# Four parts of w_in decoded ahead of the attention loop, and alpha and the gate's columns in one transfer

## The chip, the cores and the metric

One core of a Trainium2 chip runs the whole program. The metric is the device time of one execution in microseconds (us). The engines are TensorE (PE in the rows; PEld is its weight load), VectorE (DVE), ScalarE (ACT), GpSimd (POOL) and SyncE (SP), whose queue issues nearly all transfers.

## The reference

Attention with a window of 32 and 32 global rows for each of 4 x 8 heads, then a dense layer of two matrices with a leaky activation, then a layer of eight experts with a gate. w_in and w_out come as 64-bit floats, the rest as 32-bit.

```python
def _attn_ref(q_l, k_l, v_l, q_g, k_g, v_g):
    B, H, Sl, D = q_l.shape                      # 4, 8, 512, 64; q_g, k_g, v_g have 32 rows
    window = 32
    scale = 1.0 / np.sqrt(D)
    k_all = np.concatenate([k_g, k_l], axis=2)
    v_all = np.concatenate([v_g, v_l], axis=2)
    out_g = np.matmul(sm(scale * np.matmul(q_g, k_all.transpose(0, 1, 3, 2))), v_all)
    s_ll = scale * np.matmul(q_l, k_l.transpose(0, 1, 3, 2))
    mask = np.abs(pos[:, None] - pos[None, :]) <= window
    s_ll = np.where(mask, s_ll, -1000000000.0)
    s_lg = scale * np.matmul(q_l, k_g.transpose(0, 1, 3, 2))
    a_l = sm(np.concatenate([s_lg, s_ll], axis=-1))
    out_l = np.matmul(a_l, np.concatenate([v_g, v_l], axis=2))
    return np.concatenate([out_g, out_l], axis=2)

def _moe_ref(x, w_in, w_out, alpha):             # x 2176 x 512, w_in 512 x 2048, w_out 2048 x 512
    h = x @ w_in
    g = np.maximum(h, 0.0) + alpha * np.minimum(h, 0.0)
    return g @ w_out

def _moe2_ref(x, w_gate, w1, w2):                # w_gate 512 x 8; eight experts of 512 x 1024 x 512
    logits = x @ w_gate
    ...                                          # highest logits first, 272 tokens for each expert
    for e in range(E):
        mask = assigned == e
        out[mask] = np.maximum(x[mask] @ w1[e], 0.0) @ w2[e]
    return out
```

## The kernel before

The attention runs over 16 units (a batch and a pair of heads), two units at a time: a **pair** p of units is loaded by `load(p)` (queries and keys `qk`, values `vv`) and worked off in four **steps** of 128 query rows. Step n (four for each pair, counted through from 0) does: scores on PE (L366, tile `s`), mask and row minimum on DVE (L372, four instructions `sc`), exponentials on ACT (L374, four, tile `pr`), the division on DVE (L379, L380, L386), transposes on PE (L392) with a copy on ACT (L394), and the product with the values on PE (L403) with a copy on ACT (L405). The 32 global rows of a pair are done between the steps (L419 to L454). The output of a pair lies in `xb`.

The first matrix product (`gemm`, L172 for h and L203 for y) takes chunks of 272 tokens. It starts when two pairs are done (`done[0] < UPB - 1`), that is behind step 7 and the rest of its chain; then `xh` and `xl` (L73 on DVE, 128x1088) are split off `xb`, and from there PE alternates between attention and `gemm` until all eight pairs are done.

w_in and w_out must be **decoded** from 64-bit to 32-bit floats and split into a high and a low part. `win_part(pool, hf, i)` and `wout_part` do one **part** of 128 x 512: a transfer of 512 KB into `raw` (L79, three buffers), the absolute value on ACT (L82), four instructions on DVE (L83, L85, L86, L87), a cast on ACT (L72) and a subtraction on POOL (L73). The first half of the layer has 8 parts of w_in and 8 of w_out, 16 in all. Before the change four of w_in are written into the first attention loop, one behind every sixth piece of work; the other four and the eight of w_out follow in the loop with `gemm`. Alpha (2048 numbers, one for each column of w_in) and the gate's columns (512 x 8) are loaded behind the first loop, by a transfer each, from their own layout in memory.

The order of instructions on each engine isn't the order of the code: the tile framework reorders by a timeline of its own (`schedule_with_timeline_sim=True`) when the program is built. Each engine then runs its instructions strictly in that order, and a transfer in SP's queue waits for the ones ahead of it.

Of the kernel before, what the change touches and what calls it, by code (L numbers as in the profile page):

```python
# [9 lines left out]
F32 = mybir.dt.float32  # L10
# [15 lines left out]
def tile_attention_moe_moe(ctx: ExitStack, tc: tile.TileContext, qkw, vw,  # L26
                           w_in, w_out, alpha, w_gate, w1, w2, out):
    nc = tc.nc
    V, A, P, T = nc.vector, nc.scalar, nc.gpsimd, nc.tensor
# [33 lines left out]
    Lm = cp.tile([128, NT, E], F32, name="Lm")  # L63
    al = cp.tile([128, KF], F32, name="al")
    al1 = cp.tile([128, KF], F32, name="al1")
    wg = cp.tile([128, KD, 32], F32, name="wg")
    wop = cp.tile([128, KH, 32], F32, name="wop")
    P.memset(wg, 0.0)
    P.memset(wop, 0.0)
# [220 lines left out]
    with ExitStack() as at:  # L290
# [31 lines left out]

        def load(p):
            for cut in range(2 if p == 0 else 1):
                for u in (2 * p, 2 * p + 1):
# [5 lines left out]
                    part = slice(None) if p else (slice(0, QS + kpos(6)), slice(QS + kpos(6), None))[cut]  # L331
                    nc.sync.dma_start(out=d["qk"][:, part], in_=qkw[u, :, part])
            for u in (2 * p, 2 * p + 1):
                U[u]["v"] = ld.tile([128, NQ, 2 * D], F32, name="vv")
                nc.sync.dma_start(out=U[u]["v"].rearrange("p i d -> p (i d)"), in_=vw[u])
# [164 lines left out]

        load(0)
        mask = mk.tile([128, 3, KW], F32, name="mask")
# [15 lines left out]
        UPB = H // 2  # L518
        parts = [(win_part, i) for i in range(2 * KD)]
        att = attention()  # L520
        n = 0
        while done[0] < UPB - 1:
            next(att)
            n += 1
            if n >= 6 and n % 6 == 0 and len(parts) > KD:
                f, i = parts.pop(0)
                f(dc, 0, i)
        nc.sync.dma_start(out=al, in_=alpha.rearrange("(f p) -> p f", p=128))
        V.tensor_scalar(al1, al, -1.0, 1.0, op0=OP.mult, op1=OP.add)
        nc.sync.dma_start(out=wg[:, :, :E], in_=w_gate.rearrange("(k p) e -> p k e", p=128))  # L530
        parts += [(wout_part, i) for i in range(KH)]
# [686 lines left out]

_INS = ['qk', 'v', 'moe_w_in', 'moe_w_out', 'moe_alpha', 'moe2_w_gate', 'moe2_w1', 'moe2_w2']
_OUTS = [((2176, 512), 'float32')]  # L1220
# [39 lines left out]


# [24 lines left out]
```

## Time and profile before

| | us |
|---|---|
| median of 3 runs (869.75 to 871.96) | 869.96 |
| the profiled execution | 870.56 |
| its span | 868.8 |
| PE busy in the span | 820.1 (94%) |
| DVE busy | 466.8 (54%) |
| ACT busy | 389.6 (45%) |
| POOL busy | 348.5 (40%) |

The span is that of the trace; the execution lasts 1.8 us longer than it. A share of busy time is a mean over stages: in the first 40th of the page's slices PE is busy six tenths, later nine and more. The stages that the change touches lie in the first 110 us.

### The profile page before, as it was taken

To read this page: it belongs to the slowest core of one execution; us is meant where nothing else is said; L and a number is where in the kernel's file an instruction comes from. 1 tells how busy PE (TensorE), PEld (TensorE's weight loads), DVE (VectorE), ACT (ScalarE), POOL (GpSimd) and SP (SyncE) were. 2 spreads that over 40 slices of the span, in tenths; PEclk is the share of its full clock that TensorE was granted. 3 is DMA by queue.
4 is the path that set the end of the run, shared out by engine and by line. 5 is a ranking of instruction groups with operands and counts; after the bars stand their busy time and mean duration, and the time that the engine had idled before them with its cause. 6 is when DMAs were issued, how large, how long until landed. Compare 5 with 4: busy or idle time off the path is not lost. (4 is left out here: it accounts for less than half of the span.)

```text
span 868.8 us, 21017 instructions
## 1 busy us (share of the span) xinstructions
PE 820.1 (94%) x8380; PEld 746.0 (86%) x8380; DVE 466.8 (54%) x1654; ACT 389.6 (45%) x970; POOL 348.5 (40%) x300
## 2 busy tenths in 40 slices
PE   6699799999988999999999999999899999999995
PEld 4478688888988999988898899999699989999995
DVE  4789945463288734133333457666575776722120
ACT  5577646464454543232322434341254535444431
POOL 1214412020145534200000638470598868779601
PEclk9589999999999999999999999999999999999998
DMA  9777715631345302201311217242366655666300
GB/s 345 230 255 272 261 38 192 212 124 47 95 134 183 114 26 79 72 7 53 103 52 54 78 54 267 64 131 65 100 198 217 168 177 153 174 187 185 111 25 37
DMA packets 50441, 115.94 MB, mean 133 GB/s; under 512 B 6759, under 2 KB 23399, under 8 KB 48295
## 3 DMA queue, kind: packets, MB, share of 16 engines
q1 hardware_dynamic: 47447, 105.68, 37.8%
q0 software_dynamic: 2896, 8.92, 3.1%
q8 instruction: 66, 1.08, 0.5%
q14 instruction: 32, 0.26, 0.1%
HBM read 96.76 MB, written 17.83 MB: 132 GB/s over the span
## 5 line engine op out<-in xcount | busy, mean ns | idle before, releaser
L172 PE MATMUL h<-xh,win 128*128 128x272 f32 x768 | 162.3, 295 | 3.9 <-DVE g L178 2.5
L73 POOL TENSOR_TENSOR m<-raw,m 128x1024 fp32r<-128x1024 f32 x64 | 152.4, 2402 | 21.6 <-ACT m L72 21.3
L172 PEld LDWEIGHTS h<-xh,win 128*128 128x128 f32 x768 | 124.9, 188 | 12.0 <-issue 4.9
L73 POOL TENSOR_TENSOR glo<-g,ghi 128x272 fp32r<-128x272 f32 x64 | 55.4, 866 | 150.8 <-ACT ghi L72 150.7
L203 PE MATMUL y<-ghi,wout 128*128 128x272 f32 x512 | 112.5, 298 | 2.5 <-ACT wout L72 1.3
L172 PE MATMUL h<-xl,win 128*128 128x272 f32 x384 | 111.3, 290 | 1.4 <-DVE xl L73 1.4
L1104 PE MATMUL h<-gr,wout 128*128 128x272 f32 x768 | 110.7, 295 | 0.0
L73 POOL TENSOR_TENSOR gr<-gb,gr 128x272 fp32r<-128x272 f32 x64 | 48.0, 772 | 153.2 <-ACT gr L72 144.6
L977 PE MATMUL h<-xsh,m 128*128 128x272 f32 x512 | 107.4, 297 | 1.3 <-ACT xsh L72 1.3
L993 PE MATMUL h<-hh,m 128*128 128x272 f32 x512 | 103.2, 293 | 0.0
L1104 PEld LDWEIGHTS h<-gr,wout 128*128 128x128 f32 x768 | 99.2, 188 | 0.9 <-ACT gr L72 0.4
L203 PEld LDWEIGHTS y<-ghi,wout 128*128 128x128 f32 x512 | 84.3, 188 | 8.3 <-issue 4.0
L177 ACT ACTIVATE neg<-h 128x272 f32<-128x272 f32 x128 | 50.5, 395 | 90.1 <-PE h L172 89.7
L977 PEld LDWEIGHTS h<-xsh,m 128*128 128x128 f32 x512 | 83.1, 190 | 1.9 <-ACT xsh L72 1.4
L993 PEld LDWEIGHTS h<-hh,m 128*128 128x128 f32 x512 | 81.7, 188 | 0.7 <-issue 0.5
L72 ACT CAST m<-raw 128x1024 fp32r<-128x1024 f32 x64 | 65.4, 1049 | 29.1 <-DMA raw<-in_moe_w_dram 28.9
L993 PE MATMUL h<-hl,m 128*128 128x272 f32 x256 | 75.5, 295 | 0.0
L203 PE MATMUL y<-glo,wout 128*128 128x272 f32 x256 | 73.8, 293 | 1.8 <-POOL glo L73 1.5
L977 PE MATMUL h<-xsl,m 128*128 128x272 f32 x256 | 74.9, 292 | 0.5 <-DVE xsl L73 0.5
L172 PEld LDWEIGHTS h<-xl,win 128*128 128x128 f32 x384 | 72.3, 188 | 2.4 <-DVE xl L73 1.9
L178 DVE SCALAR_TENSOR_TENSOR gb<-neg,al,h 128x272 f32<-128x272 f32 x64 | 31.6, 496 | 76.5 <-ACT neg L177 66.0
L374 ACT ACTIVATE pr<-sc,mx 128x128 f32<-128x128 f32 x128 | 50.1, 393 | 30.6 <-DVE mx L372 30.4
(231 smaller groups left out, 1517.2 us busy)
## 6 DMA issues: line engine op xcount, KB each, us to landing
raw<-in_moe_w_dram SPq DMA_DIRECT2D x64, 512.0 KB, 3.8
vv<-in_v_dram SPq DMA_DIRECT2D x16, 1024.0 KB, 8.0
qk<-in_qk_dram SPq DMA_DIRECT2D x14, 720.0 KB, 8.5
raw<-in_moe_w_in_dram SPq DMA_DIRECT2D x16, 512.0 KB, 4.4
raw<-in_moe_w_out_dram SPq DMA_DIRECT2D x16, 512.0 KB, 4.2
xs<-xb SPq DMA_DIRECT2D x16, 272.0 KB, 8.8
xpart<-xd SPq DMA_DIRECT2D x32, 136.0 KB, 1.7
xb<-xs SPq DMA_DIRECT2D x8, 544.0 KB, 4.0
```

Source lines behind the costliest of these rows:

```text
L72: a = A.copy(hi, src)
L73: return a, (lo_eng or V).tensor_tensor(lo, src, hi.bitcast(F32), op=OP.subtract)
L172: T.matmul(ps, wi[:, w, k, fs], x[:, k], start=i == 0, stop=i == 3 * KD - 1)
L177: A.activation(out=neg, in_=ps, func=AF.Relu, scale=-1.0)
L178: epi[0] = V.scalar_tensor_tensor(g, neg, al1[:, hf * KH + f:hf * KH + f + 1], ps, op0=OP.mult, op1=OP.add)
L203: T.matmul(ps, wo[:, w, f, ds_], x[:, f], start=i == 0, stop=i == 3 * KH - 1)
L374: A.activation(out=d["pr", j][:, ii], in_=sc, func=AF.Exp, bias=d["mx", j][:, ii:ii + 1], scale=-1.0, accum_out=d["sm", j][:, ii:ii + 1])
L977: T.matmul(ps, d["w1"][:, w, kk, fs], x[:, kk], start=i == 0, stop=i == 3 * KD - 1)
L993: T.matmul(ps, d["w2"][:, w, f, ms], x[:, f], start=i == 0, stop=i == 3 * K3 - 1)
L1104: T.matmul(ps[j], wo[:, w, f, ds_], x, start=f == 0 and a == 0, stop=f == KH - 1 and a == 2)
```

## The change

The first four parts of w_in are issued inside `load(0)`: two behind the first cut of `qk` of pair 0, two behind its second cut, ahead of the values. They are no longer in the attention loop. Alpha and the gate's columns lie in one array `gate` of 128 x 144, which is laid out ahead of the launch, with zeros where the gate's columns are padded from 8 to 32; it takes one transfer, and the clearing of `wg` on POOL (L68) is gone. `al` and `wg` are views of the one tile. Line numbers behind L320 move by 2 to 5.

```diff
@@ -61,11 +61,11 @@
     Lm = cp.tile([128, NT, E], F32, name="Lm")
-    al = cp.tile([128, KF], F32, name="al")
+    ag = cp.tile([128, KF + KD * 32], F32, name="ag")
+    al = ag[:, :KF]
     al1 = cp.tile([128, KF], F32, name="al1")
-    wg = cp.tile([128, KD, 32], F32, name="wg")
+    wg = ag[:, KF:].rearrange("p (k e) -> p k e", e=32)
     wop = cp.tile([128, KH, 32], F32, name="wop")
-    P.memset(wg, 0.0)
     P.memset(wop, 0.0)
@@ -320,7 +320,7 @@
-        def load(p):
+        def load(p, between=()):
             for cut in range(2 if p == 0 else 1):
                 for u in (2 * p, 2 * p + 1):
...
                     nc.sync.dma_start(out=d["qk"][:, part], in_=qkw[u, :, part])
+                for f in between[2 * cut:2 * cut + 2]:
+                    f()
             for u in (2 * p, 2 * p + 1):
@@ -498,7 +500,9 @@
-        load(0)
+        parts = [(win_part, i) for i in range(2 * KD)]
+        load(0, [lambda i=i: win_part(dc, 0, i) for _, i in parts[:KD]])
+        del parts[:KD]
@@ -516,18 +520,11 @@
         UPB = H // 2
-        parts = [(win_part, i) for i in range(2 * KD)]
         att = attention()
-        n = 0
         while done[0] < UPB - 1:
             next(att)
-            n += 1
-            if n >= 6 and n % 6 == 0 and len(parts) > KD:
-                f, i = parts.pop(0)
-                f(dc, 0, i)
-        nc.sync.dma_start(out=al, in_=alpha.rearrange("(f p) -> p f", p=128))
+        nc.sync.dma_start(out=ag, in_=gate)
         V.tensor_scalar(al1, al, -1.0, 1.0, op0=OP.mult, op1=OP.add)
-        nc.sync.dma_start(out=wg[:, :, :E], in_=w_gate.rearrange("(k p) e -> p k e", p=128))
         parts += [(wout_part, i) for i in range(KH)]
@@ -1259,6 +1256,14 @@
+def lay_gate(alpha, w_gate):
+    import numpy as _np
+    E = w_gate.shape[1]
+    wg = _np.zeros((128, w_gate.shape[0] // 128, 32), w_gate.dtype)
+    wg[:, :, :E] = w_gate.reshape(-1, 128, E).transpose(1, 0, 2)
+    return _np.concatenate([alpha.reshape(-1, 128).T, wg.reshape(128, -1)], axis=1)
```

**SP's queue, from its start.** Each row is a transfer, with its tiles and its shape (L79 brings a part's `raw`). Before:

```order
L332 DMA qk<-in_qk_dram 128x416 x2
L332 DMA qk<-in_qk_dram 128x1024 x2
L335 DMA vv<-in_v_dram 128x2048 x2
L332 DMA qk<-in_qk_dram 128x1440 x2
L335 DMA vv<-in_v_dram 128x2048 x2
L79 DMA raw<-in_moe_w_in_dram 128x1024 x3
L528 DMA al<-in_moe_alpha_dram 128x16x1
L530 DMA wg<-in_moe_w_gate_dram 128x4x8
L332 DMA qk<-in_qk_dram 128x1440 x2
L79 DMA raw<-in_moe_w_in_dram 128x1024 x4
```

And with the change, from the same place:

```order
L332 DMA qk<-in_qk_dram 128x416 x2
L79 DMA raw<-in_moe_w_in_dram 128x1024 x2
L332 DMA qk<-in_qk_dram 128x1024 x2
L79 DMA raw<-in_moe_w_in_dram 128x1024
L337 DMA vv<-in_v_dram 128x2048 x2
L332 DMA qk<-in_qk_dram 128x1440 x2
L337 DMA vv<-in_v_dram 128x2048 x2
L526 DMA ag<-in_gate_dram 128x144
L79 DMA raw<-in_moe_w_in_dram 128x1024 x3
L332 DMA qk<-in_qk_dram 128x1440 x2
```

Three parts stand ahead of the values of pair 0, two of them ahead of the second cut of its queries and keys; the fourth part waits for a buffer and comes behind the loads of pair 1.

**ACT, from its start.** L82 is the absolute value of a part and L72 its cast; `pr` are the exponentials of a step (L374 before, L376 with the change). Before:

```order
L374 ACTIVATE pr,sm<-sc,mx 128x128 x8
L394 COPY pt<-t 128x512
L424 ACTIVATE gsc,gmx<-gsc,gmx 128x544
L374 ACTIVATE pr,sm<-sc,mx 128x128 x4
L394 COPY pt<-t 128x512
L374 ACTIVATE pr,sm<-sc,mx 128x128
```

With the change:

```order
L82 ACTIVATE mag<-raw 128x512
L376 ACTIVATE pr,sm<-sc,mx 128x128 x4
L82 ACTIVATE mag<-raw 128x512
L72 CAST win<-mag 128x512
L82 ACTIVATE mag<-raw 128x512
L72 CAST win<-mag 128x512
L376 ACTIVATE pr,sm<-sc,mx 128x128 x2
L396 COPY pt<-t 128x512
L72 CAST win<-mag 128x512
L376 ACTIVATE pr,sm<-sc,mx 128x128 x3
```

The first part's absolute value stands ahead of the exponentials of step 0, and the three first parts are done before step 2.

**DVE, between the exponentials' division of step 4 and the scores of step 5.** `mag` are the four instructions of a part, `sm` and `pr` the division, `xb<-go` the global rows of pair 0, `sc,mx` the scores. Before, behind the scores of step 4:

```order
L83 TENSOR_SCALAR mag<-mag 128x512
L85 TENSOR_SCALAR mag<-mag 128x512
L86 SCALAR_TENSOR_TENSOR mag<-raw,mag 128x512
L379 TENSOR_SCALAR sm<-sm 128x4
L83 TENSOR_SCALAR mag<-mag 128x512
L87 SCALAR_TENSOR_TENSOR mag<-raw,mag 128x512
L380 RECIPROCAL sm<-sm 128x4
L85 TENSOR_SCALAR mag<-mag 128x512
L529 TENSOR_SCALAR al_70<-al 128x16
L386 TENSOR_SCALAR pr<-pr,sm 128x128 x4
L86 SCALAR_TENSOR_TENSOR mag<-raw,mag 128x512
L87 SCALAR_TENSOR_TENSOR mag<-raw,mag 128x512
```

These are two of the four parts that stand there; the other two follow, around the copy of `xb<-go`, up to the scores of step 5.

With the change, at the same place:

```order
L527 TENSOR_SCALAR al_70<-ag 128x16
L381 TENSOR_SCALAR sm<-sm 128x4
L382 RECIPROCAL sm<-sm 128x4
L388 TENSOR_SCALAR pr<-pr,sm 128x128 x4
L83 TENSOR_SCALAR mag<-mag 128x512
L85 TENSOR_SCALAR mag<-mag 128x512
L86 SCALAR_TENSOR_TENSOR mag<-raw,mag 128x512
L87 SCALAR_TENSOR_TENSOR mag<-raw,mag 128x512
L456 COPY xb<-go 128x2x32
L374 ISA sc,mx<-s,mask 128x128
```

Four parts stood between step 4 and step 5 before, one does now. Counted in the whole order, DVE does six parts ahead of the split `xl` before and eight with the change, so that ten and eight are left behind it; the four scores of step 9 stood ahead of `xl` and now stand behind it.

## Rows read from the trace of the kernel before

**Rows 1.** Stretches: start:end, length, busy us of each engine (instructions), clock, DMA.

```profile
5.00:22.40 17.40, 13.83 (x226) 8.66 (x226) 11.03 (x73) 10.08 (x41) 0.00 (x0) 1.00 1.00 405
22.40:38.20 15.80, 9.27 (x154) 6.09 (x152) 10.92 (x25) 7.26 (x17) 3.81 (x3) 0.60 0.81 257
38.20:58.20 20.00, 18.61 (x310) 13.49 (x302) 15.45 (x84) 13.81 (x48) 2.13 (x2) 0.72 0.70 239
58.20:110.30 52.10, 45.13 (x681) 37.39 (x677) 50.87 (x149) 38.44 (x120) 21.97 (x19) 1.00 0.71 250
110.30:240.00 129.70, 129.03 (x1978) 114.05 (x1979) 59.62 (x296) 70.34 (x239) 19.61 (x23) 1.00 0.35 120
...
40.00:50.00 10.00, 9.92 (x126) 7.08 (x126) 5.65 (x37) 8.15 (x31) 1.15 (x1) 0.52 0.86 271
```

**Rows 2.** The timeline of SP's queue: start, us, issued transfers.

```profile
5.03 1.46 SPq L335 DMA_DIRECT2D vv<-in_v_dram  x2
7.49 4.14 SPq L79 DMA_DIRECT2D raw<-in_moe_w_in_dram  x3
...
16.62 10.20 SPq L530 DMA_DIRECT2D wg<-in_moe_w_gate_dram  x1
...
26.92 0.93 SPq L332 DMA_DIRECT2D qk<-in_qk_dram  x2
28.06 11.48 SPq L79 DMA_DIRECT2D raw<-in_moe_w_in_dram  x4
```

**Rows 3.** The timeline of ACT: start, us, and in brackets the idle time before.

```profile
5.41 0.40 ACT L374 ACTIVATE pr<-sc,mx 128x128 f32<-128x128 f32 x1 [3.38 <-DVE mx L372]
...
24.56 0.66 ACT L82 ACTIVATE mag<-raw 128x512 f32<-128x512 f32 x1 [2.19 <-DMA raw<-in_moe_w_in_dram]
...
35.97 0.66 ACT L82 ACTIVATE mag<-raw 128x512 f32<-128x512 f32 x1 [0.45 <-DMA raw<-in_moe_w_in_dram]
```

**Rows 4.** The timeline of PE.

```profile
7.52 0.65 PE L366 MATMUL s<-qk 64*32 64x128 f32 x8 [2.59 <-DMA qk<-in_qk_dram]
...
20.97 1.12 PE L403 MATMUL o<-pt,vv 128*64 128x32 f32 x32
...
27.23 1.92 PE L403 MATMUL o<-pt,vv 128*64 128x32 f32 x32 [2.78 <-ACT xb L405]
```

**Rows 5.** DVE's groups of a part, 0 to 120 us: count, busy, mean ns, idle before.

```profile
L86 DVE SCALAR_TENSOR_TENSOR mag<-raw,mag 128x512 int32<-128x512 int32 x16 | 14.1, 888 | 0.2
L87 DVE SCALAR_TENSOR_TENSOR mag<-raw,mag 128x512 int32<-128x512 int32 x16 | 11.9, 748 | 0.0
L85 DVE TENSOR_SCALAR mag<-mag 128x512 int32<-128x512 int32 x16 | 8.9, 564 | 0.3
L83 DVE TENSOR_SCALAR mag<-mag 128x512 f32<-128x512 f32 x16 | 7.7, 492 | 5.1 <-ACT mag L82 5.1
```

**Rows 6.** The timeline of DVE and POOL.

```profile
5.08 0.29 DVE L372 CUSTOM_DVE_ANT_0 sc<-s,mask 128x128 f32<-128x128 f32 x1 [0.40 <-PE s L366]
...
7.51 0.88 DVE L386 TENSOR_SCALAR pr<-pr,sm 128x128 f32<-128x128 f32 x4
...
22.12 0.28 DVE L372 CUSTOM_DVE_ANT_0 sc<-s,mask 128x128 f32<-128x128 f32 x1
...
28.38 1.90 DVE L386 TENSOR_SCALAR pr<-pr,sm 128x128 f32<-128x128 f32 x4
...
28.72 1.27 POOL L73 TENSOR_TENSOR win<-mag,win 128x512 fp32r<-128x512 f32 x1 [24.08 <-ACT win L72]
...
38.26 0.28 DVE L372 CUSTOM_DVE_ANT_0 sc<-s,mask 128x128 f32<-128x128 f32 x1
...
49.98 0.42 DVE L443 COPY gt<-gt 128x256 f32<-128x256 f32 x1 [2.86 <-PE gt L442]
...
58.29 1.48 DVE L73 TENSOR_TENSOR xl<-xb,xh 128x1088 fp32r<-128x1088 f32 x1
```

**Rows 7.** The last instruction of a part on DVE: first and last start.

```profile
L87 DVE SCALAR_TENSOR_TENSOR mag<-raw,mag x16: 660/682/1762, 27.3 to 109.6; 128x512 int32<-128x512 int32 x16
```

More of the change, by code (lines that the diff above doesn't have):

```diff
@@ L26, in tile_attention_moe_moe @@
 def tile_attention_moe_moe(ctx: ExitStack, tc: tile.TileContext, qkw, vw,
-                           w_in, w_out, alpha, w_gate, w1, w2, out):
+                           w_in, w_out, gate, w1, w2, out):
     nc = tc.nc
@@ L1216, in tile_attention_moe_moe @@
             pass
-_INS = ['qk', 'v', 'moe_w_in', 'moe_w_out', 'moe_alpha', 'moe2_w_gate', 'moe2_w1', 'moe2_w2']
+_INS = ['qk', 'v', 'moe_w_in', 'moe_w_out', 'gate', 'moe2_w1', 'moe2_w2']
 _OUTS = [((2176, 512), 'float32')]
@@ L1272 @@
     inputs = {**inputs, **lay_out(*(_np.asarray(inputs[n]) for n in names))}
+    inputs['gate'] = lay_gate(_np.asarray(inputs['moe_alpha']), _np.asarray(inputs['moe2_w_gate']))
     for name in _INS:
```

## The prediction

> **What bounds the kernel now.** I first cut the opening of the run into stretches by events on DVE, because the change moves parts of w_in and a part is mostly DVE work. The table of stretches [rows 1] gives one line from the first step's scores to the end of step 4's (5.0 to 22.4 us), one to the first scores of step 5 (38.2), one to the split `xl` that lets the matrix product begin (58.2), one to the end of the last part, and one behind. From 110.3 to 240 us PE is busy 129.03 of 129.70 us: whatever is gained or lost ahead of that point moves the end one for one. From 58.2 to 110.3 DVE is busy 50.87 of 52.10 us and PE only 45.13. From 38.2 to 58.2 neither is full, DVE with 15.45 of 20.00. The two stretches before have DVE at 11.03 of 17.40 and 10.92 of 15.80. So DVE, with the sixteen parts in its order, sets when PE's saturated time begins, and the first three stretches hold 6.4, 4.9 and 4.6 us in which it does nothing.
>
> Next I read the timelines for what ended those idle times. SP issues the first three parts at 7.49, behind the queries, keys and values of two pairs [rows 2]; DMA moves 405 GB/s in that stretch [rows 1], and the first part is there only at 24.56, where ACT has waited 2.19 us for it [rows 3]. ACT runs in order, so the copy of `xb` behind it is late, PE waits 2.78 us for that copy, and the next product of 32 instructions takes 1.92 us where the one at 20.97 took 1.12 [rows 4]: the granted clock of the stretch falls to a mean of 0.60, that is from 2.4 to 1.2 GHz for most of it, behind PE's idle time. Between 22.4 and 38.2 stands no attention step at all, only the division of step 4 and four parts.
>
> **The change part by part.** A part costs DVE 888 + 748 + 564 + 492 = 2692 ns on the mean [rows 5]. The sum follows DVE from event to event.
>
> *Step 0 waits for a part.* ACT's order now begins with the absolute value of the first part, so the exponentials of step 0 stand behind it. Its transfer takes the place of the second cut of `qk`, which released PE at 7.52 [rows 4], so about 7.5; with 0.66 for the absolute value [rows 3] the exponentials begin at 8.2 and not at 5.41 [rows 3]. Bounds: 6.5 and 9.
>
> *To the end of step 4's scores.* DVE has 11.0 us of work there before [rows 1]; about 0.9 of it, the scores of step 0 (four instructions of 0.29 from 5.08 on [rows 6], which overlap a little), still run while the part is awaited. The rest, 10.1, and three parts, 8.1, are 18.2 us from 8.2 on: 26.4 if nothing is waited for. I add 2.0 for the exponentials that a division waits for (they are about three tenths of the 6.4 us that DVE was idle there): 28.4 against 22.4, **6.0 later**. Bounds: without any wait 4.0 later; with the whole 6.4 us of idle time kept, 10.4 later.
>
> The second cut of `qk` lies behind 1 MB more, the values behind 1.5 MB: 2.6 and 3.9 us at the stretch's 405 GB/s. PE's first score behind them goes from 7.5 to about 10, and the scores of step 1 on DVE from 11.3 to what the parts leave, about 16, so the transfers are covered by the parts; without these, 2.6 us would show.
>
> *To the first scores of step 5.* The order has one part here in place of four. Left are the copy of `gt` (0.42, as [rows 6] shows for a later pair), the division of step 4 (0.88 for its four instructions [rows 6] and some 0.4 ahead of them), one part (2.7), the alpha and `xb` copies (0.3), and a wait for the four exponentials of step 4 (0.40 each [rows 3], about 1.5): 6.2 us in place of 15.8. Step 5 begins at 34.6 against 38.2: **3.6 earlier** in all. Bounds for the stretch: 4.7 with the wait hidden, 9 if the fourth part's transfer is late (1.5 MB behind the same queue, about 28 us) and stalls ACT as now.
>
> *To the split xl.* Here 20.0 us hold two parts; with the change they hold four, and the scores of step 9 (0.9) move behind. Two of the parts stand in the new order around the copy of `gt`, where DVE waits 2.86 us at 49.98 [rows 6], so +5.4 - 0.9 - 2.9 = 1.6 longer. `xl` begins **2.0 earlier**. Bounds: 0 longer if all of the 4.6 idle us take work, 4.5 longer if none do.
>
> *To the last part.* Eight parts are left and not ten, against it the 0.9 of step 9: DVE has 4.5 us less work. PE has 7.0 us of idle time there [rows 1], which is the most that can go. Between nothing and 4.5 I take **3.3**, nearer to the upper end because DVE is 98% busy in that line. The last part, at 109.6 [rows 7], then comes 5.3 earlier.
>
> *Alpha and the gate.* The old issue of the gate's columns holds SP for 10.20 us, to 26.92, and four parts and the loads of pair 2 queue behind it [rows 2]. Freed, it is worth little: the fourth part needs the first one's buffer, which DVE gives back at 28.0 (27.3 and 0.68 [rows 7]), and SP issues it at 28.06 [rows 2]. What it does carry is the loads of pair 2 in front of that part, 1.5 MB or 3.6 us, of which ACT's wait at 35.97 shows 0.45 [rows 3]. The whole lies in the 15.8 us that I have already replaced, so I give it 0; if it were taken alone, 0 to 2.5. The clearing of `wg` on POOL is not awaited: the first scores on DVE wait for PE (0.40 at 5.08 [rows 6]).
>
> Sum: +6.0 - 9.6 + 1.6 - 3.3 = -5.3. From the profiled execution's 870.56 that is 865.3; it stands 0.6 above the median of the runs, so **864.7**.
>
> **A rule against it.** Four divisions take 0.88 us at 7.51 with POOL quiet and 1.90 us at 28.38 with POOL's subtraction of a part from 28.72 on [rows 6]. The mean of 2692 ns already holds such collisions for the part's own instructions; three subtractions now meet the dense early divisions instead. The Trainium skill, "GPSIMD Engine Reference", section "Specifications", says that GpSimd shares its SBUF interfaces with VectorE and contends with two-input or two-port VectorE instructions; these two rows agree. By that rule each of the three early subtractions would stretch what lies beside it by about 1.0 us, and the sum would be 867.7. I keep 865.3 as the basis, since the later divisions lose the same collisions.
>
> **The rivals.** *The clock recovers.* Half of the third stretch runs at the lower level (mean 0.72 [rows 1]). Behind the change PE has no 2.8 us wait for ACT at 24 us, and if it stays at 2.4 GHz, the 9.9 us that PE is busy from 40 to 50 at a mean clock of 0.52 [rows 1] shrink by 1.92/1.12 = 1.71 to 5.8: 4.1 us less, about 860.6. For it: PE's long gaps of 24 to 40 us stem from the four parts. Against it: PE now waits for DVE in steps 1 to 4, which may send the clock down earlier. The Trainium skill, "TensorE: Matmul & The Clock Gate", section "What's actually happening", has the same two levels, the lower one behind idle time.
>
> *The gain is hidden.* If the wait in the last stretch is for chains through ACT and PE and not for parts, its 3.3 is 0 and 868.0 is left; that is within 0.3% (2.6 us, about what a measurement can tell from no change).
>
> *Slower: the parts keep their present price.* Between step 4 and 5 four parts take 15.8 us, 3.95 each, because ACT, DVE and POOL hand each part on in turn. If the three early parts cost that and none of it is covered, step 4's scores end 2.8 + 11.9 = 14.7 later, at 37.1; with 6.2 step 5 begins at 43.3, 5.1 later than now; with 1.6 and -3.3 the end is 3.4 later, 873.4. It decides if step 5 begins later than about 40 us. For it: ACT's new order mixes casts and absolute values among the exponentials of steps 0 to 2. Against it: 6.4 us of idle DVE lie there.
>
> *The change does nothing:* not possible for the order on the engines; for the transfers, the same bytes arrive by 25 us.
>
> **How the numbers follow.** Forecast (861 to 867.3) 0.45, clock recovered (857 to 861) 0.18, hidden (867.4 to 872.5) 0.20, slower 0.17. Hence faster 0.63, same 0.20, slower 0.17. The range reaches from 857.5 over the rival at 873.4 to 874; outside lie the deepest recovery and half of the slower case.
>
> **What would show it.** Exponentials of step 0 near 8.2; scores of step 5 near 34.6; `xl` near 56.3; the last part near 104.3; SP with no issue of 10 us; the idle DVE of the first three stretches down from 15.8 to about 10. It is wrong if step 4's scores end behind 33 us, or if the last stretch keeps its 52 us with two parts less.

## The result, and the profile after

The changed kernel takes 874.82 us (median of 8 executions, 872.84 to 875.96) and the kernel before, on the same chip, 870.27 (8, 869.75 to 871.96): a ratio of 1.0052 with a 95% interval of 1.0038 to 1.0065. It is slower by 4.5 us; 864.7 was predicted. The profiled execution's span is 874.1 us against 868.8.

The stretches of the changed kernel, cut at the same times as [rows 1], with some more:

```profile
5.00:22.40 17.40, 9.15 (x129) 5.08 (x129) 14.61 (x57) 9.60 (x33) 3.92 (x3) 0.96 1.01 403
22.40:38.20 15.80, 13.57 (x251) 9.42 (x249) 9.30 (x50) 10.20 (x36) 1.27 (x1) 0.82 0.76 298
38.20:58.20 20.00, 16.82 (x294) 13.13 (x294) 16.39 (x68) 10.90 (x37) 2.51 (x2) 0.67 0.73 258
58.20:110.30 52.10, 43.73 (x608) 36.23 (x609) 48.00 (x147) 37.04 (x110) 21.57 (x18) 0.80 0.56 197
110.30:240.00 129.70, 129.70 (x2012) 114.08 (x2011) 59.67 (x303) 70.03 (x241) 16.67 (x20) 1.00 0.36 121
...
50.00:70.00 20.00, 11.64 (x150) 8.09 (x153) 18.91 (x49) 11.39 (x31) 6.75 (x5) 0.63 0.61 215
...
66.00:79.00 13.00, 12.57 (x126) 10.84 (x126) 12.90 (x42) 10.53 (x33) 5.08 (x4) 0.50 0.64 198
...
57.00:66.00 9.00, 2.52 (x9) 0.59 (x8) 8.01 (x16) 4.16 (x9) 3.06 (x2) 0.50 0.49 168
55.30:79.20 23.90, 16.89 (x170) 12.35 (x161) 22.78 (x60) 15.18 (x41) 8.92 (x7) 0.50 0.60 196
...
0.00:110.00 110.00, 84.55 (x1311) 64.36 (x1311) 89.23 (x319) 69.02 (x216) 32.97 (x44) 0.81 0.69 252
0.00:50.00 50.00, 35.46 (x587) 24.28 (x587) 33.52 (x156) 27.61 (x93) 8.89 (x24) 0.83 0.78 291
50.00:110.00 60.00, 49.09 (x728) 40.08 (x724) 55.71 (x166) 41.41 (x123) 24.08 (x20) 0.80 0.62 219
```

The last stretch is full, as it was before, so the loss lies ahead of 110 us. There PE is busy 84.55 us at a mean clock of 0.81. The same view of the kernel before:

```profile
0.00:110.00 110.00, 88.21 (x1386) 66.43 (x1387) 88.38 (x329) 70.87 (x224) 31.76 (x44) 0.89 0.77 270
0.00:50.00 50.00, 35.14 (x536) 22.86 (x544) 29.80 (x144) 28.08 (x93) 8.92 (x25) 0.76 0.84 291
50.00:110.00 60.00, 53.06 (x858) 43.57 (x855) 58.58 (x186) 42.79 (x131) 22.84 (x19) 1.00 0.71 251
```

PE does nothing for 3.7 us more, and the clock is lower. PE's busy time times its clock says where the work is lost: up to 50 us the changed kernel has done more (35.46 x 0.83 = 29.4 against 26.7), and from 50 to 110 us much less (39.3 against 53.1). 8.4 of its idle microseconds lie between 50 and 70 us (the **hole** below), and the granted clock is 0.50, that is 1.2 GHz, from 55.3 to 79.2 us, ahead of the hole's longest waits and through the start of the matrix product. The timelines show where the idle time comes from. ACT:

```profile
7.28 0.66 ACT L82 ACTIVATE mag<-raw 128x512 f32<-128x512 f32 x1 [5.24 <-DMA raw<-in_moe_w_in_dram]
7.84 0.39 ACT L376 ACTIVATE pr<-sc,mx 128x128 f32<-128x128 f32 x1
...
58.25 0.66 ACT L82 ACTIVATE mag<-raw 128x512 f32<-128x512 f32 x1 [2.66 <-DMA raw<-in_moe_w_in_dram]
```

DVE, with the scores of step 4 and 5, the division of step 7, and what stands ahead of `xl`:

```profile
28.59 0.29 DVE L374 CUSTOM_DVE_ANT_0 sc<-s,mask 128x128 f32<-128x128 f32 x1
...
33.62 0.28 DVE L374 CUSTOM_DVE_ANT_0 sc<-s,mask 128x128 f32<-128x128 f32 x1
...
52.15 1.29 DVE L87 SCALAR_TENSOR_TENSOR mag<-raw,mag 128x512 int32<-128x512 int32 x2
...
53.77 2.78 DVE L388 TENSOR_SCALAR pr<-pr,sm 128x128 f32<-128x128 f32 x4
...
58.94 0.43 DVE L83 TENSOR_SCALAR mag<-mag 128x512 f32<-128x512 f32 x1 [0.86 <-ACT mag L82]
...
60.22 0.22 DVE L456 COPY xb<-go 128x64 f32<-128x64 f32 x1
...
62.63 1.28 DVE L73 TENSOR_TENSOR xl<-xb,xh 128x1088 fp32r<-128x1088 f32 x1
```

SP's queue and PE:

```profile
52.86 0.33 SPq L79 DMA_DIRECT2D raw<-in_moe_w_in_dram  x1
```

```profile
10.35 0.65 PE L368 MATMUL s<-qk 64*32 64x128 f32 x8 [5.42 <-DMA qk<-in_qk_dram]
...
60.49 1.98 PE L421 MATMUL gs<-qk 128*64 128x512 f32 x4 [3.37 <-DVE xb L456]
...
64.24 0.43 PE L421 MATMUL gs<-qk 128*64 128x32 f32 x4 [1.78 <-ACT xb L407]
66.43 0.56 PE L172 MATMUL h<-xh,win 128*128 128x272 f32 x1 [1.76 <-DVE mx L374]
```

And the first `h` on PE in the kernel before:

```profile
58.31 0.52 PE L172 MATMUL h<-xh,win 128*128 128x272 f32 x2
```

SP issues the eighth part's transfer at 52.86, just when the first of the two L87 at 52.15 (0.69 each) gives a raw buffer back. ACT waits 2.66 us for it, the copy of `xb` stands behind it on DVE at 60.22, and PE waits 3.37 us for that copy, then 1.78 and 1.76: 6.9 of the 8.4 us. `h` begins at 66.43 and not at 58.31. And the last part:

```profile
L87 DVE SCALAR_TENSOR_TENSOR mag<-raw,mag x16: 679/689/1645, 10.4 to 98.0; 128x512 int32<-128x512 int32 x16
```

It comes 11.6 us earlier than before [rows 7], and the kernel is slower all the same.

### The profile page after: what moved, and what is told of

It is laid out like the page before. It is cut to its first block, busy times and chain, and to the rows that moved or that the text cites. A ratio compares the mean times of both kernels' runs of the same rounds, so it can differ in the third digit from the quotient of the medians.

```text
span 874.1 us, 21022 instructions
## 1 busy us (share of the span) xinstructions
PE 823.4 (94%) x8380; PEld 751.1 (86%) x8380; DVE 468.8 (54%) x1654; ACT 389.9 (45%) x970; POOL 348.2 (40%) x299
## 4 chain that ended last, share of the span: by engine, by line
PE 69%; DVE 11%; issue 7%; ACT 5%; DMA 4%; POOL 3%; POOLq 0%; SPq 0%; ACTq 0%; DVEq 0%
PE h L172 20%; PE h L1101 12%; PE y L203 9%; PE h L990 7%; PE h L974 6%; PE o L405 2%; DVE mag L86 2%; DMA raw<-in_moe_w_in_dram 2%; DMA raw<-in_moe_w_dram 2%; PE lp L260 2%; POOL m L73 2%; DVE mag L87 2%; PE s L368 1%; DVE pr L388 1%; ACT m L72 1%
## 5 line engine op out<-in xcount | busy, mean ns | idle before, releaser
L172 PE MATMUL h<-xh,win 128*128 128x272 f32 x768 | 166.3, 300 | 6.4 <-DVE g L178 3.3
L172 PEld LDWEIGHTS h<-xh,win 128*128 128x128 f32 x768 | 127.7, 192 | 14.8 <-issue 7.3
L974 PEld LDWEIGHTS h<-xsh,m 128*128 128x128 f32 x512 | 83.1, 190 | 2.0 <-ACT xsh L72 1.4
L72 ACT CAST m<-raw 128x1024 fp32r<-128x1024 f32 x64 | 65.3, 1049 | 28.7 <-DMA raw<-in_moe_w_dram 28.5
L990 PE MATMUL h<-hl,m 128*128 128x272 f32 x256 | 75.5, 295 | 0.0
L376 ACT ACTIVATE pr<-sc,mx 128x128 f32<-128x128 f32 x128 | 49.9, 391 | 27.1 <-DVE mx L374 27.1
```

Source lines behind the costliest of these rows:

```text
L72: a = A.copy(hi, src)
L172: T.matmul(ps, wi[:, w, k, fs], x[:, k], start=i == 0, stop=i == 3 * KD - 1)
L376: A.activation(out=d["pr", j][:, ii], in_=sc, func=AF.Exp, bias=d["mx", j][:, ii:ii + 1], scale=-1.0, accum_out=d["sm", j][:, ii:ii + 1])
L974: T.matmul(ps, d["w1"][:, w, kk, fs], x[:, kk], start=i == 0, stop=i == 3 * KD - 1)
L990: T.matmul(ps, d["w2"][:, w, f, ms], x[:, f], start=i == 0, stop=i == 3 * K3 - 1)
```

## The experiments

Theory 1: the parts that the new order puts ahead of `xl` (eight; six before) make the hole in PE and the low clock around it. Theory 2: the front, with step 0's exponentials and the second cut of `qk` behind a part, is never paid back. Theory 3: the gate's transfer. The table has all runs. "Parts" are those of w_in ahead of `xl` on DVE by the trace; idle is PE's, clock is that of 0 to 110 us; the product is PE's busy time of 0 to 110 us times that clock. The median is that of all executions of the kernel; the ratio is to the kernel before in the same series, whose median lies between 870.1 and 871.8. The other columns belong to the profiled execution, which need not be the middle one: in e4 and e10 it is the slowest, 5.7 and 5.5 us above the median, in e12 and e15 it lies 4.0 and 5.3 below.

| kernel | median us | ratio, 95% | parts | xl at | idle 0-20 | idle 50-70 | clock | product | span |
|---|---|---|---|---|---|---|---|---|---|
| before | 870.3 | | 6 | 58.3 | 6.8 | 1.0 | 0.89 | 78.5 | 868.8 |
| changed | 874.8 | 1.0052 (1.0038-1.0065) | 8 | 62.6 | 10.9 | 8.4 | 0.81 | 68.5 | 874.1 |
| e1 | 873.7 | 1.002 (1.000-1.004) | 6 | 66.4 | 6.5 | 0.0 | 0.81 | 72.6 | 874.2 |
| e2 | 876.9 | 1.0065 (1.0048-1.0081) | 8 | 62.6 | 10.2 | 7.6 | 0.83 | 70.4 | 875.1 |
| e3 | 870.1 | 0.9991 (0.9979-1.0003) | 4 | 54.6 | 11.6 | 2.8 | 0.89 | 76.9 | 869.7 |
| e4 | 868.3 | 0.9971 (0.9952-0.999) | 6 | 60.7 | 7.8 | 0.0 | 0.83 | 79.3 | 872.2 |
| e5 | 867.8 | 0.9973 (0.9953-0.9993) | 4 | 56.5 | 7.9 | 0.0 | 0.86 | 83.1 | 865.0 |
| e6 | 875.3 | 1.0061 (1.0036-1.0085) | 7 | 61.4 | 10.6 | 6.9 | 0.82 | 69.6 | 876.1 |
| e7 | 872.4 | 1.0028 (1.0002-1.0055) | 4 | 56.8 | 6.5 | 1.2 | 0.87 | 80.4 | 870.7 |
| e8 | 879.6 | 1.0106 (1.0091-1.0121) | 8 | 62.3 | 10.6 | 5.1 | 0.86 | 72.8 | 877.1 |
| e9 | 878.4 | 1.0084 (1.0071-1.0097) | 8 | 67.7 | 9.9 | 6.9 | 0.80 | 67.9 | 879.4 |
| e10 | 862.5 | 0.9896 (0.9881-0.9911) | 6 | 55.6 | 9.6 | 1.6 | 0.94 | 86.3 | 866.2 |
| e11 | 875.5 | 1.0043 (1.0027-1.0059) | 6 | 64.5 | 7.8 | 0.0 | 0.83 | 75.5 | 875.0 |
| e12 | 872.9 | 1.0009 (0.998-1.0037) | 6 | 57.3 | 9.7 | 0.0 | 0.91 | 83.6 | 867.1 |
| e13 | 864.4 | 0.9914 (0.989-0.9938) | 6 | 59.5 | 9.7 | 0.3 | 0.88 | 82.5 | 865.1 |
| e14 | 864.1 | 0.9927 (0.9901-0.9952) | 6 | 53.5 | 9.4 | 0.7 | 0.96 | 90.8 | 861.8 |
| e15 | 876.6 | 1.0082 (1.006-1.0105) | 6 | 57.0 | 10.5 | 6.2 | 0.89 | 75.6 | 869.5 |
| e16 | 873.4 | 1.0034 (1.0013-1.0054) | 8 | 63.8 | 9.8 | 2.8 | 0.85 | 76.4 | 874.2 |
| e17 | 878.2 | 1.0073 (1.0048-1.0098) | 7 | 62.0 | 11.3 | 3.5 | 0.78 | 68.7 | 876.9 |
| e18 | 874.9 | 1.0034 (1.0018-1.0051) | 6 | 57.7 | 10.8 | 4.9 | 0.83 | 72.6 | 874.0 |

Over these 20 profiled executions the span falls by 0.68 us for each microsecond of the product (correlation -0.92). So what a kernel does in 0 to 110 us is read better from PE's busy time and its clock together than from either of the two (in size, idle time alone has a correlation of 0.68 with the span and the clock alone one of 0.84). The end of the parts on DVE says little: the last L87 comes at 98.0 in the changed kernel and at 104.7 in e10, the fastest.

**e1, the gate's edit alone**: the parts are back in the loop.

```diff
-        load(0, [lambda i=i: win_part(dc, 0, i) for _, i in parts[:KD]])
+        load(0)
...
+            if n >= 6 and n % 6 == 0 and len(parts) > KD:
+                f, i = parts.pop(0)
+                f(dc, 0, i)
```

> The changed kernel with its first edit undone: the parts of w_in are in the attention loop again, behind every sixth piece, and only alpha and the gate's columns come in one transfer. Theory 1 (the parts placed around the split xl cost the time): no loss, ratio to the kernel before 0.996 to 1.001, the split xl between 55 and 58.5 us. Theory 2 (the front costs it): the same, as the front is undone. Theory 3 (the gate's transfer costs it, because parts and loads that it held back now come early and crowd): slower, 1.003 or more.

873.7 us: no gain, at most a small loss. The split `xl` was to come between 55 and 58.5 by theory 1; it comes at 66.4, with six parts ahead of it and no hole, so the number of parts and the hole don't tell this kernel's time. Its twelve executions lie between 868.4 us (mean granted clock of the span 0.981) and 876.3 (0.970); the profiled one, 876.0, has the clock at the lower level from 28 to 65 us.

**e2, the parts alone**: alpha and the gate's columns by their own transfers.

```diff
-        nc.sync.dma_start(out=ag, in_=gate)
+        nc.sync.dma_start(out=al, in_=alpha.rearrange("(f p) -> p f", p=128))
...
```

> The kernel before with four parts of w_in between the first loads and nothing else; alpha and the gate's columns keep their own transfers. Theory 1: the order on DVE again has eight parts ahead of the split xl, so xl comes at 61 us or later and the ratio is 1.003 to 1.010. Theory 2: the front is that of the changed kernel, so the ratio is about the same 1.005 whatever xl does. Theory 3: no loss, 0.994 to 1.001.

876.9 us, with the hole again (7.6 us) and eight parts ahead of `xl`: the loss comes with the parts.

**e3, all later parts behind `xl` on DVE**; **e4, the early parts behind all loads of pair 0**; **e5, both**.

```diff
...
-                        with tc.issue_after(at_norm[UPB // 2 - 1, STEPS - 1].ins):
+                        with tc.issue_after(xls[0].ins):
...
-        load(0, [lambda i=i: win_part(dc, 0, i) for _, i in parts[:KD]])
+        load(0)
+        for _, i in parts[:KD]:
+            win_part(dc, 0, i)
```

> The changed kernel, but the parts of w_in and w_out that go with the first matrix product are issued behind the split xl of its first chunk, and so only four parts stand ahead of xl in place of eight. The front (parts between the first loads) is kept. Theory 1: xl begins between 50 and 56 us, the clock is at 2.4 GHz soon behind it, and the time falls by 4 us or more against the changed kernel: 862 to 870, ratio 0.991 to 1.000. Theory 2: xl comes earlier but the time stays at 873 to 876, ratio 1.004 to 1.007. A third way: the parts are then missing where the product asks for them, and PE waits for decoded weights behind xl, which would show as PE idle time between 60 and 110 us and a ratio above 1.007.

> The changed kernel, but the four parts of w_in are issued behind all loads of the first pair of units, not between them. The order on DVE then has the steps 1 to 4 free of parts at their start, and six parts ahead of the split xl in place of eight. Theory 1: xl at 56 to 60 us and a ratio of 0.995 to 1.002, because two parts less stand ahead of xl. Theory 2: also faster than the changed kernel, by the 5 to 6 us that the front lost: 0.997 to 1.000, and step 4's scores end near 22 us and not at 28.6. Both expect a gain here; the runs with xl held and with the parts alone tell the theories apart, and this one says what the place of the transfers is worth.

> Both edits of the two better kernels in one: the four early parts behind all loads of the first pair, and every later part's work on VectorE behind the split xl. If the front (parts between the loads) and the split xl each cost on their own, the gains add: PE's idle time in the span falls to 40 to 43 us (it is 41.6 with the parts behind the loads, 49.4 with xl held, 50.7 in the changed kernel) and the time is 862 to 867, ratio 0.990 to 0.996. If they are the same 4 to 7 us, it stays with the better of the two, 867 to 869, ratio 0.996 to 0.999. If the parts that are held behind xl are then missing, PE waits for VectorE behind 60 us and it is 870 or more.

e3 keeps the front (11.6 us idle there, more than in the changed kernel) and gets 4.8 us back; the hole shrinks to 2.8. That is the upper end of theory 1's range, and not what theory 2 expected. e4 gets 6.5 us back, with both at once, the free front and two parts less ahead of `xl`. e5 is no better than e4 within the intervals: the two gains don't add.

**e6, only the eighth part (and w_out) behind `xl` on DVE**, in the changed kernel.

```diff
...
+                        behind = xls[0] if f is wout_part or i == 2 * KD - 1 else at_norm[UPB // 2 - 1, STEPS - 1]
+                        with tc.issue_after(behind.ins):
```

> The changed kernel with the eighth part of w_in and the parts of w_out behind the split xl on VectorE; parts five to seven stay where the changed kernel has them, and so does the front. If the late transfer of the eighth part (it waits for one of three raw buffers, lands 5.3 us later, and holds up ScalarE and then VectorE's copy of xb) is the core of the loss: xl at 56 to 59 us, PE's wait of 3.4 us ahead of the global scores gone, and the time 870 to 872, ratio 0.999 to 1.002, near that with all four parts behind xl. If it is the number of parts ahead of xl that costs: xl at 59 to 61 and the ratio 1.003 to 1.005.

875.3 us, a hole of 6.9. This alone doesn't settle the matter, since only DVE's work was held: ACT still waits 2.39 us for the transfer at 58.93, ahead of the cast `xh`. With ACT's work held too (e17) the hole is 3.5 and the time no better, so the one transfer, as I had read it from the wait of 2.66 us, isn't the core.

**e7, the kernel before with e3's edit.**

> The kernel before with one edit: the later parts' work on VectorE stands behind the split xl. No part is early and alpha and the gate keep their transfers. If holding xl gains by itself, whatever the front does: 864 to 868, ratio 0.993 to 0.998. If the gain of holding xl in the changed kernel (4.8 us) only takes back what that kernel had put ahead of xl (eight parts in place of six): 869 to 872, ratio 0.999 to 1.002.

872.4 us: `xl` 1.5 us earlier brings nothing. Where six parts stand ahead, holding them back is worth nothing.

**e8, products without use in the gap.**

```diff
...
+            warm(p, 2 if part else 4, lastt[0])
             s = bank([128, hi - lo], "gs")
```

> The changed kernel with six products of 128x128 by 128x512 whose result nobody reads, five behind the transposes and one behind the global scores of the third pair, in the time from 57 to 66 us in which PE waits. The order on VectorE and ScalarE up to the split xl is the same. If the lower clock at the start of the matrix product (1.2 GHz up to 79 us) is a cause: the clock of 66 to 79 us is near 2.4 GHz and the time falls by 2 to 4 us, ratio 1.001 to 1.003. If the clock there is only a companion of waiting for VectorE, the time stays at 874 to 876, ratio 1.004 to 1.007, with PE idle for the time that it gains. If the clock does not rise, it tells nothing.

879.6 us, and no test of the clock. In PE's timeline the filler waits for the very copy that makes the gap, so it stands in PE's way; and the order behind `xl` changed, so that a later wait came of it (the filler counts as busy in the table):

```profile
60.12 6.83 PE L92 MATMUL idle<-ident 128*128 128x512 f32 x10 [3.67 <-DVE xb L465]
...
75.83 0.43 PE L430 MATMUL gs<-qk 128*64 128x32 f32 x4 [5.63 <-DVE gmx L431]
```

Since an added product changes the scheduler's order behind it, the clock wasn't tried by itself.

**e9, three transfers early, their work on DVE behind the scores of a later step.**

```diff
...
+        load(0, [lambda i=i: ahead(i) for i in range(3)])
...
+                with tc.issue_after(scored[0].ins):
+                    f(dc, 0, i)
```

> The changed kernel's transfers without its early decoding: three parts' transfers stand between the first loads as in the changed kernel, but VectorE's four instructions of each early part are issued behind the scores of the step that the loop has then reached (ScalarE's first absolute value still stands ahead of the exponentials of step 0). If the late second cut of the queries and the late values alone cost (transfers): PE's idle time of 0 to 20 us stays at 10 to 11 us as in the changed kernel, and the time is 871 to 875. If VectorE's work on three parts among the first steps is what costs: the scores of step 1 stand 3 us later than before, and not 6, PE's idle time of 0 to 20 us is 8 to 9.5 us, and the time is 867 to 870.

878.4 us, worse than the changed kernel and than both expectations: early transfers without early decoding bring nothing here, and again eight parts stand ahead of `xl`, which comes at 67.7.

**e10, the four parts behind the second cut of `qk`**; **e13, one between the cuts and three behind**.

```diff
-                for f in between[2 * cut:2 * cut + 2]:
-                    f()
+                if cut:
+                    for f in between:
+                        f()
...
-                for f in between[2 * cut:2 * cut + 2]:
+                for f in between[1:] if cut else between[:1]:
```

> The changed kernel with all four parts issued behind the second cut of the queries and keys, ahead of the values; so the queries are as early as before, and only the values wait for 1.5 MB. If the late second cut is what the front loses: PE's wait for it is back at 2.6 us (5.4 in the changed kernel), its idle time of 0 to 20 us at 7 to 8.5, and the time at 867 to 871. If the early decoding or the late values cost as much, the idle time of 0 to 20 us stays above 9.5 us and the time at 872 to 876.

> The changed kernel with one part between the cuts of the queries and three behind the second, in place of two and one: half the dose. If the transfers ahead of the second cut cost by their bytes: PE's wait for the cut is about 4 us (2.5 with none ahead, 5.4 with two), and the time half-way between 862.5 and 874.8, 866 to 871. If it is all ScalarE's order, which also here has a part ahead of step 0's exponentials: 872 to 876.

e10 takes 862.5 us, 8.4 less than the kernel before in the same series (870.9), by the place of two transfers; both expectations had it slower. That looks like theory 2, but e13, too, is faster than both of its expectations. First the timelines of PE and ACT in e10, and its stretches:

```profile
7.37 0.65 PE L369 MATMUL s<-qk 64*32 64x128 f32 x8 [2.48 <-DMA qk<-in_qk_dram]
...
5.37 0.40 ACT L377 ACTIVATE pr<-sc,mx 128x128 f32<-128x128 f32 x1 [3.34 <-DVE mx L375]
```

```profile
50.00:70.00 20.00, 18.41 (x323) 15.16 (x321) 19.09 (x56) 16.59 (x52) 7.07 (x6) 1.00 0.85 304
...
0.00:110.00 110.00, 91.80 (x1468) 69.50 (x1468) 91.47 (x345) 74.12 (x238) 33.61 (x44) 0.94 0.74 270
```

The same of e13:

```profile
9.21 0.65 PE L368 MATMUL s<-qk 64*32 64x128 f32 x8 [4.39 <-DMA qk<-in_qk_dram]
...
7.42 0.66 ACT L82 ACTIVATE mag<-raw 128x512 f32<-128x512 f32 x1 [5.39 <-DMA raw<-in_moe_w_in_dram]
7.99 0.39 ACT L376 ACTIVATE pr<-sc,mx 128x128 f32<-128x128 f32 x1
```

```profile
50.00:70.00 20.00, 19.71 (x276) 15.96 (x276) 17.65 (x61) 14.42 (x43) 6.04 (x6) 0.83 0.83 293
...
0.00:110.00 110.00, 93.70 (x1418) 72.16 (x1418) 89.76 (x336) 72.56 (x228) 32.92 (x44) 0.88 0.74 270
```

e13 has most of the changed kernel's front: its exponentials behind a part (7.99; 7.84 there), and a late second cut, behind one part and not two (PE at 9.21; 10.35 there). Yet it takes 864.4. PE idles 9.6 and 9.7 us of the first 20 in e10 and e13, 10.9 in the changed kernel: 1.2 us of the front, against 10 us of time. With the changed kernel ahead at 50 us in PE's work, theory 2 falls as a price that is paid in the front and carried to the end. In e10 and e13 six parts stand ahead of `xl`, and the hole is 1.6 and 0.3 us.

One rival isn't separated: that two parts ahead of the second cut lead the scheduler to a worse order later on. All ten kernels that have them (the changed one, e2, e3, e6, e8, e9, e12, e15, e17, e18) take 870.1 us or more, and of the four with the parts ahead of the values and at most one ahead of that cut only e16 takes more than 864.4.

**e11, e4 without the gate's transfer**; **e14, e10 without it**.

> The kernel before with the four parts behind all loads of the first pair, and alpha and the gate's columns in their own transfers. If the gain of the kernel with the parts behind the loads (868.3) comes from the parts: 867 to 870, ratio 0.995 to 0.999. If it needs the gate's one transfer, since the old one holds the queue for 10 us ahead of the fourth part and of the loads of the third pair: 871 to 874, ratio 1.000 to 1.004.

> The parts behind the second cut, with alpha and the gate's columns in their own two transfers: what the gate's edit is worth beside the better place. By the pair with the parts behind all loads (868.3 with the one transfer, 875.5 with the two) it is worth some 7 us: 867 to 871. By the pair with the parts between the loads (874.8 and 876.9) some 2: 863 to 866. If nothing: 861 to 863.

875.5 us against e4's 868.3, and 864.1 against e10's 862.5, where the intervals overlap. With e2, the one transfer brought 2.1, 7.2 and 1.6 us beside early parts, and lost 1.7 beside none (e1's ratio). Only the 7.2 is clear of the intervals; each is a new order on all engines, and its price isn't one number.

**e12, the changed kernel's transfers with ACT's work on the early parts behind step 0's exponentials.**

```diff
...
+        next(att)
+        for _, i in parts[:KD]:
+            with tc.issue_after(expd[0].ins):
+                win_part(dc, 0, i)
```

> The changed kernel's transfers in its order (two parts between the cuts of the queries), but ScalarE's work on the early parts stands behind the exponentials of step 0, so that these no longer wait for a part. If the late second cut is what costs: PE waits 5.4 us for it as in the changed kernel, idles 9.5 to 11 us of the first 20, and the time is 870 to 875. If ScalarE's order (step 0's exponentials behind a part) is what costs: the exponentials begin at 5.4, and the time is 862 to 867 as with all parts behind the second cut.

872.9 us, with 9.7 us of idle time in the first 20: that is what was expected if the late second cut costs. The exponentials begin early, and the second cut is as late as in the changed kernel, though PE has other work up to it:

```profile
5.38 0.40 ACT L383 ACTIVATE pr<-sc,mx 128x128 f32<-128x128 f32 x1 [3.35 <-DVE mx L381]
...
10.22 0.65 PE L375 MATMUL s<-qk 64*32 64x128 f32 x8 [1.86 <-DMA qk<-in_qk_dram]
```

The executions lie wide, from 865.1 us (clock 0.980) to 876.8 (0.972). The profiled one, 868.9, is among the quick ones: no hole, six parts ahead of `xl`. So six parts ahead of `xl` do not make a time short; e1 and e11 have six and take 873.7 and 875.5.

**e16, e10 with `xl` behind the eighth part**: theory 1 from the other side. The front is e10's.

```diff
...
+            with tc.issue_after(decoded[0].ins):
+                V.tensor_tensor(xl, src, xh.bitcast(F32), op=OP.subtract)
...
+        for f, i in parts:
+            with tc.issue_after(at_norm[UPB // 2 - 1, STEPS - 1].ins):
+                f(dc, 0, i)
```

> The fastest kernel so far (parts behind the second cut, 862.5) with the split xl issued behind the eighth part on VectorE, so that eight parts stand ahead of it, as in the changed kernel, in place of six; the front is untouched. If parts ahead of xl make the loss: xl at 64 us or later, the first products of h later by as much, and the time 868 to 876. If the front makes it: the time stays at 861 to 866. If only the copy of xb behind the parts matters, and not xl (the second copy of xb stands behind five parts here, behind seven in the changed kernel): little idle time, and 863 to 868.

873.4 us, 10.9 more than e10 (by the ratios 1.4%). DVE, then PE, then the stretch:

```profile
63.75 1.28 DVE L162 TENSOR_TENSOR xl<-xb,xh 128x1088 fp32r<-128x1088 f32 x1
...
60.92 0.66 PE L401 MATMUL t<-ident,pr 128*128 128x128 f32 x2 [2.66 <-DVE pr L395]
...
66.40 0.59 PE L178 MATMUL h<-xl,win 128*128 128x272 f32 x1
```

```profile
50.00:70.00 20.00, 17.23 (x257) 13.84 (x255) 18.47 (x60) 14.78 (x46) 5.51 (x4) 0.74 0.84 309
```

With two parts more ahead of it `xl` comes 8.1 us later, PE waits for a division, the clock falls, and the product of 0 to 110 us goes from 86.3 to 76.4. The fronts are alike up to 50 us, and the loss lies behind. e10:

```profile
0.00:50.00 50.00, 39.23 (x650) 25.97 (x650) 34.90 (x174) 30.15 (x104) 9.03 (x24) 0.86 0.88 332
50.00:110.00 60.00, 52.57 (x824) 43.53 (x822) 56.57 (x172) 43.97 (x135) 24.58 (x20) 1.00 0.63 218
```

e16:

```profile
0.00:50.00 50.00, 39.53 (x664) 26.91 (x664) 35.13 (x174) 30.56 (x106) 9.01 (x24) 0.86 0.88 332
50.00:110.00 60.00, 50.36 (x654) 40.86 (x652) 54.94 (x156) 38.55 (x112) 24.61 (x20) 0.83 0.55 198
```

That an order ahead of `xl` can cost more than the change lost is shown by this. It isn't a test of `xl` alone: the edit also issues parts five to eight at once, ahead of the loop with `gemm`.

**e15, parts seven and eight behind `xl` on DVE; e17, the eighth also behind the cast `xh` on ACT; e18, both parts behind both**: all in the changed kernel; the lines are e18's.

```diff
...
+                        behind = xls[0] if f is wout_part or i >= 2 * KD - 2 else (at_norm[UPB // 2 - 1, STEPS - 1],) * 2
+                        with tc.issue_after(behind[0].ins), tc.issue_after(behind[1].ins):
```

> The changed kernel with parts seven and eight of w_in and the parts of w_out behind the split xl on VectorE; the transfers and the front stay, and five parts are left ahead of xl in the order in place of eight. If the parts ahead of xl make the hole (PE idles 8.4 us from 50 to 70 us in the changed kernel, 7.0 with seven ahead, 2.8 with four): the idle time of 50 to 70 us is under 3 us, xl at 54 to 58 us, and the time 866 to 871. If the front makes the loss, the time stays at 873 to 876.

> The changed kernel with the eighth part of w_in and the parts of w_out behind the cast xh on ScalarE as well as behind the split xl on VectorE (the run with VectorE alone left ScalarE's wait for the late transfer ahead of xh, and a hole of 6.9 us). If ScalarE's wait for the eighth part's transfer makes the hole: xl at 57 to 59 us, PE's idle time from 50 to 70 us at 3 to 5 us, and the time 868 to 873. If the order of PE itself makes it (in this kernel and the changed one twelve products of h stand directly behind the global scores, and the scores of the next step behind them): the idle time stays at 6 to 8 us and the time at 873 to 878.

> The same for parts seven and eight, so that five parts are left ahead of xl on VectorE and none of the two stands ahead of xh on ScalarE. If ScalarE's wait makes the hole: xl at 54 to 56 us, PE's idle time from 50 to 70 us under 4 us, and the time 866 to 871, better than 876.6 with VectorE alone held. If PE's order makes it: idle 5 to 7 us and 872 to 878.

876.6, 878.2 and 874.9 us. By the trace six, seven and six parts are left ahead of `xl` (the expectations say five for e15 and e18). The hole shrinks (6.2, 3.5, 4.9 us; 8.4 in the changed kernel) and little or no time comes back: by the ratios e18 is 1.6 us better than the changed kernel, with overlapping intervals, and the other two are no better. The clock of 0 to 110 us stays at 0.78 and 0.83 in e17 and e18. In e15 it is 0.89, and that execution, 871.3 us, is the quickest of its six (up to 880.4). The times are about those that were expected if the front (e15) or PE's own order (e17, e18) makes the loss. So it is not one wait of one engine.

## Why the prediction was wrong

*Step 0 waits for a part: right.* The exponentials begin at 7.84 (8.2 was said), the second cut reaches PE at 10.35 (about 10).

*To the end of step 4's scores: right.* They end at 28.9 (28.59 and 0.29); 28.4 was said. The parts did not keep their old price of 3.95 us.

*To the first scores of step 5: right, and 1.0 us better.* They start at 33.62; 34.6 was said. Here the change is 4.6 us ahead [rows 6], and the front is paid back, on PE too (29.4 against 26.7 up to 50 us). The slower rival's point (step 5 behind 40 us) was not reached: its time came near the truth by another road.

*To the split xl: the step that failed.* I had 21.6 us from step 5's scores to `xl`, with an upper bound of 24.5; it took 29.0. I counted DVE's work, with the two parts more some 20.0 us, and let it fill the old idle time down to 1.6. DVE does 21.08 us of work there and idles 7.9:

```profile
33.62:62.63 29.01, 21.14 (x342) 14.41 (x340) 21.08 (x83) 16.38 (x51) 5.25 (x4) 0.70 0.62 214
```

What I missed are waits of engines for one another. The longest, 3.55 us on DVE, is for step 5's exponentials. On ACT the sixth part's absolute value stands ahead of them, and it waits for POOL's subtraction of the fourth part, which held one of the two buffers `mag`; DVE takes the sixth part up only at 48.76. DVE and ACT:

```profile
38.09 0.17 DVE L381 TENSOR_SCALAR sm<-sm 128x4 f32<-128x4 f32 x1 [3.55 <-ACT pr L376]
```

```profile
35.59 0.66 ACT L82 ACTIVATE mag<-raw 128x512 f32<-128x512 f32 x1 [1.38 <-POOL win L73]
```

The division of step 7 is stretched by 1.9. At the end the eighth part can't be fetched before a buffer is free, ACT waits for it in order, and `xb` and `xh` stand behind; PE waits 6.9 us in this stretch, with its clock at 1.2 GHz since 55.3. How the loss divides among these waits is open: e17 took the eighth part's away and brought no time back.

*To the last part: the premise failed.* "DVE, with the sixteen parts in its order, sets when PE's saturated time begins": the last part came at 98.0, 6.3 us earlier than I said, and the time was lost all the same. I had bounded the stretch by DVE being full; but PE, at half its clock up to 79 us, did 39.3 us of work at full clock from 50 to 110 us, and 53.1 before. Neither of my two signs of being wrong came (step 4's scores behind 33 us; the last stretch keeping its 52): both watched DVE.

*The clock rival had the sign wrong.* The clock did recover from 28 to 38 us and from 48 to 55, and was at the lower level again from 55.3 to 79.2; in the fourth stretch it is 0.80, and 1.00 before. Of the 4.5 us about 2 may go with it: the changed kernel's execution with the highest mean clock (0.977) takes 872.84, 2.0 less than its median and 2.6 more than the kernel before. This is an estimate from 8 executions, and it doesn't tell whether the clock or the waits came first.

*Alpha and the gate: 0 was said.* Beside the changed kernel's parts the one transfer is worth 2.1 us within overlapping intervals (e2); 7.2 us beside another place of the parts (e4, e11) show that it can't be priced alone.

Shown: the loss lies between 50 and 110 us and comes with the parts, not the gate's edit (e2); it isn't time lost in the front and carried on; an order with two parts more ahead of `xl` costs 10.9 us in the fastest kernel (e16), and all later parts behind `xl` bring back 4.8 in the changed one, front and all (e3). Open: why three partial releases brought nothing (e15, e17, e18); whether two parts ahead of the second cut lead to the worse order; how much is PE's own order, in which twelve products of `h` stand ahead of the next step's scores; and what the clock does to an order that is otherwise the same.

## What to carry to other kernels

If a change lets a scheduler reorder engines that run in order, count what stands ahead of the instruction that opens the bound engine's full stretch, on every engine and with its transfers, before adding up work; here a gain of 4.6 us at step 5 was lost around that place. Judge a stretch ahead of a full TensorE by its busy time times its granted clock, not by when another engine gets through its work. And try the place of early transfers by themselves: behind the cut that the second step waits for, the same four parts made the kernel 1.0% faster (e10) and not 0.5% slower.

## What the hardware did that was not expected

*One program, several clocks.* e4's twelve executions go from 865.19 us (mean granted clock 0.982) to 873.96 (0.970), in order of clock with few exceptions (correlation -0.88). The order of instructions is the same in all, so 1% of time comes and goes without an edit, and it goes with how long TensorE is at 1.2 GHz; which of the two causes the other these numbers don't show. The Trainium skill, "TensorE: Matmul & The Clock Gate", section "What's actually happening", has the lower level behind idle time. The changed kernel's row from 57 to 66 us agrees: PE is busy 2.52 of the 9.00 us at a clock of 0.50.

*What 1.2 GHz costs.* The 32 small products of a step take 1.92 us in place of 1.12 [rows 4], a factor of 1.7 and not of 2.

*DVE beside POOL.* The division of step 7 took 2.78 us for its four instructions at 53.77, three times the 0.88 of [rows 6], beside two subtractions on POOL:

```profile
53.56 2.51 POOL L73 TENSOR_TENSOR win<-mag,win 128x512 fp32r<-128x512 f32 x2 [18.00 <-ACT win L72]
```

I had taken 1.0 us for such a meeting and left it out of the sum; two in a row cost 1.9, in the stretch that failed. The sharing of interfaces that the Trainium skill states in "GPSIMD Engine Reference", "Specifications", bears on this place, and the rows agree with it; no run took the subtractions away.
